# From the third batch on, attention 1's scores are turned by VectorE and a trip through DRAM instead of by TensorE

## The chip, the cores and the metric

The program runs on one core of a Trainium2 chip. The metric is the device time of one launch in microseconds (us), the median of a few runs. A core has TensorE (PE in the profile), VectorE (DVE), ScalarE (ACT), GpSimd (POOL) and SyncE (SP, which here only issues DMAs), each with its own instruction stream that runs in order and waits on semaphores of the others.

## The reference

Eight batches, eight heads, 576 positions of width 64, and 32 "pack" queries p. Attention 1 lets the pack queries look at k and v; attention 2 lets q look at the 32 packed rows; the result goes through a two-layer feed-forward net with softplus.

```
def sm_attn(qq, kk, vv):
    s = scale * np.matmul(qq, kk.transpose(0, 1, 3, 2))
    a = np.exp(s - np.max(s, axis=-1, keepdims=True))
    a = a / (np.sum(a, axis=-1, keepdims=True) + 1e-09)
    return np.matmul(a, vv)
p_packed = sm_attn(p, k, v)                 # attention 1: [8, 8, 32, 64]
out = sm_attn(q, p_packed, p_packed)        # attention 2: [8, 8, 576, 64]
x = out.transpose(0, 2, 1, 3).reshape(4608, 512)
h = x @ w_in                                # 512 x 2048
g = np.maximum(h, 0.0) + np.log1p(np.exp(-np.abs(h)))
return g @ w_out                            # 2048 x 512
```

## The kernel before

**Units.** The feed-forward net of a batch is done in 16 units f = 0 to 15, one for each 128 columns of the hidden layer. Batches are numbered from 0, as in the tiles' names: `a_5_1` is batch 5, group 1. In a unit TensorE runs 12 products of the first layer (`gemm1`, L744, six into each of the two halves `ph_f_0` and `ph_f_1`, c = 0 and 1, of 288 columns), then four tiles of the second layer (`acc_0` to `acc_3`, L810, three products each) that belong to the unit two before. ScalarE makes Abs, Exp and Ln of each half (L770 to L772), VectorE adds max(h, 0) (`e`, L787), which also frees that half of `ph` (there are two such banks, so the next unit's `gemm1` waits for it), and then splits the result into `gh` (L756) and `gl` (L757).

**Attention in slots.** The attention of batch b is done inside the units of batch b-1. `attention_in_slots` puts each step at a place (f, t): in unit f, behind tile `acc_t` (t = 0 to 3), or at t = END, behind the whole unit. This order is written out by hand for TensorE, VectorE and ScalarE. The eight heads form two groups g of four; the scores of a group lie in `a1[g]`, 128 partitions (4 heads x 32 pack rows) x 576 positions.

For one group the steps are: `move` turns k (`T_k`) or q (`T_q`, L299, VectorE in blocks of 32 x 32); `score1` (L318) multiplies; `max1` (L343) and `exp1` (L350) on VectorE and ScalarE; `turn1` (`a1_transposed`) turns the 128 x 576 scores into `a1T`, 96 positions on the partitions, by six TensorE transposes (`psa`, L363, three to a bank, c = 0 and 1) that ScalarE copies out (L364); `pack` (L377) multiplies `a1T` by v, 24 small products for each group; `scale_pack` (`pp`, L387) and `turn_pack` (`psx`, L392, and `pt`, L394) prepare the packed rows; `score2` at (6, END) and (10, END) starts attention 2.

For batches 3 to 7 the places are: `turn1` of group 0 at (2, 0) and (2, 2); `max1` and `exp1` of group 1 at (4, 0); `turn1` of group 1 twice at (4, END); `pack` at (5, 0), `scale_pack` at (5, 1), `turn_pack` at (5, 3). Batch 2 (`LATE`) starts later: its four `turn1` stand at (4, 0), (4, 2) and twice at (4, END). Batches 0 and 1 have an order of their own.

**Loads.** SyncE issues all loads and most stores. A load waits for its buffer (four `ld` buffers serve k, v and q in turn), and what stands behind it on SyncE waits too.

Of the kernel before, what the change touches and what calls it, by code (L numbers as in the profile page):

```python
# [9 lines left out]
F32 = mybir.dt.float32  # L10
# [16 lines left out]
def pack_attention_then_softplus_ffn(  # L27
# [10 lines left out]
    nc = tc.nc  # L38
    B, H, S, D = q.shape
    J = p.shape[2]  # L40
    DM, DFF = w_in.shape
    P = 128
    NP = 96
    SI = S // NP
    HS = SI // 2
    C = S // 2
    G = H * J // P
    HG = H // G
# [5 lines left out]
    LATE = 2  # L54
# [12 lines left out]
    cv = ctx.enter_context(tc.tile_pool(name="cv", bufs=1))  # L67
    work = ctx.enter_context(tc.tile_pool(name="work", bufs=2))
    small = ctx.enter_context(tc.tile_pool(name="small", bufs=2))
    ps_acc = ctx.enter_context(tc.tile_pool(name="ps_acc", bufs=NT, space=bass.MemoryType.PSUM))  # L70
    ps_h = ctx.enter_context(tc.tile_pool(name="ps_h", bufs=2, space=bass.MemoryType.PSUM))
    ps_m = ctx.enter_context(tc.tile_pool(name="ps_m", bufs=2, space=bass.MemoryType.PSUM))
# [20 lines left out]
    def bank(nm, pool=None):  # L93
        if pool:
            return pool.tile([P, 512], F32, tag="h", name=nm)
        if spare:
            spare.append(spare.pop(0))
            pool, tag = spare[-1]
            return pool.tile([P, 512], F32, tag=tag, name=nm)
        return ps_m.tile([P, 512], F32, tag="m", name=nm)  # L100
# [20 lines left out]
    loaded = {}  # L121
    late = []

    def load(nm, b, g):
        if b >= B:
            return
        if late is not None and b == LATE:
            late.append((nm, b, g))
            return
        with tc.issue_after(last_weight.ins) if b == LATE else nullcontext():  # L130
            load_now(nm, b, g)

    def load_now(nm, b, g):

        src = {"q": q, "k": k, "v": v}[nm][b, g * HG:(g + 1) * HG]
        if b < BY_BLOCK:
            t = ld.tile([NP, HG, SI, D], F32, tag="ld", name=f"{nm}_{b}_{g}")
            nc.sync.dma_start(
                t.rearrange("x h s d -> x h (s d)"), src.rearrange("h (x s) d -> x h (s d)", s=SI)
            )  # L140
        elif nm == "v":
            t = ld.tile([NP, HG, SI, D], F32, tag="ld", name=f"{nm}_{b}_{g}")
            nc.sync.dma_start(
                t.rearrange("x h s d -> x (h s) d"), src.rearrange("h (s x) d -> x (h s) d", s=SI)
            )
        else:
            t = ld.tile([P, HG, NB, J], F32, tag="ld", name=f"{nm}_{b}_{g}")
            blocks = src.rearrange("h (n c x) (w d) -> c w x (h n) d", c=2, x=J, w=D // J)
            for o in range(P // J):
                c, w = divmod(o, D // J)  # L150
                nc.sync.dma_start(
                    t[o * J:(o + 1) * J].rearrange("x h n d -> x (h n) d"), blocks[c, w]
                )
        loaded[nm, b, g] = t
# [16 lines left out]
    def release():  # L171

        nonlocal late
        late, todo = None, late
        for x in todo:
            load(*x)

    last_weight = None
# [180 lines left out]
    def a1_transposed(b, g, c, a1, a1T, copy=nc.scalar.copy):  # L359
        ps = bank(f"psa_{b}_{g}_{c}")  # L360
        for i in range(HS):
            o = c * C + i * NP
            nc.tensor.transpose(ps[:NP, i * P:(i + 1) * P], a1[:, o:o + NP], ident)  # L363
        copy(  # L364
            a1T[:, c * HS:(c + 1) * HS, :].rearrange("x s j -> x (s j)"), ps[:NP, :HS * P]
        )

    def packed(b, g, a1T, rs):

        ps = bank(f"psp_{b}_{g}")  # L370
        pack_products(b, g, a1T, ps)
        return pack_scaled(b, g, ps, rs)

    def pack_products(b, g, a1T, ps):
        for s in range(SI):
            for hh in range(HG):
                nc.tensor.matmul(  # L377
                    ps[hh * J:(hh + 1) * J, :D],
                    a1T[:, s, hh * J:(hh + 1) * J],
                    loaded["v", b, g][:, hh, 2 * (s % HS) + s // HS if b < BY_BLOCK else s, :],  # L380
                    start=(s == 0), stop=(s == SI - 1),
                )

    def pack_scaled(b, g, ps, rs):
        pp = small.tile([P, 2, D], F32, tag="pp", name=f"pp_{b}_{g}", bufs=2)
        for i in range(2):
            nc.vector.tensor_scalar_mul(pp[:, i, :], ps[:, :D], rs)  # L387
        return pp
# [128 lines left out]
    def attention_in_slots(b):  # L517

        kT, qT = {0: [], 1: []}, {0: [], 1: []}
        a1, nm, rs, a1T, pp, a2 = {}, {}, {}, {}, {}, {}  # L520

        def at(f, t, fn, *args):
            steps.setdefault(((b - 1) * NF + f, t), []).append((fn, args))
# [21 lines left out]

        def turn1(g, c):
            if c == 0:
                pool, tag, bufs = (cv, "x", 2) if g and b >= LATE else (work, "a1T", 1)
                a1T[g] = pool.tile([NP, SI, P], F32, tag=tag, name=f"a1T_{b}_{g}", bufs=bufs)
            a1_transposed(b, g, c, a1[g], a1T[g])  # L550

        def pack():
            pp["ps"] = bank(f"psp_{b}")
            for g in range(G):
                pack_products(b, g, a1T[g], pp["ps"][:, g * D:])
# [21 lines left out]
        END = NT  # L577
        if b < LATE:
            for g in range(G):
                for hh in range(HG):  # L580
                    at(1 + 2 * g + (2 * hh + 2 * g) // NT, (2 * hh + 2 * g) % NT, move, "k", g, hh)
                    at((6 if g else 7) + (4 * g) + hh // 2, hh % 2 * 2, move, "q", g, hh)
                at(3 + 2 * g, 1, score1, g, False)
                at(3 + 2 * g, 1, load, "q", b, g)
                at(3 + g, 0, load, "v", b, g)
                at(4 + 2 * g, 0, max1, g)
                at(4 + 2 * g, 0, exp1, g)
                at(5 + 2 * g, 0, sum1, g)
            for g in range(G):
                for c in range(2):  # L590
                    at(6 + g, (g + 2 * c) % NT, turn1, g, c)
                at(7 + g, 0, pack_one, g)
                at(8, 2, load, "k", b + 1, g)
                at(9, g, turn_pack, g)
                at(9 if g == 0 else 12, 3 if g == 0 else 1, score2, g, False)
                at(9 if g == 0 else 12, 3, load, "v", b + 1, g)
            at(10, 0, exp2, 0, 0)
            at(10, 0, exp2, 0, 1)
            at(10, 3, div2, 0, 0)
            at(11, 1, div2, 0, 1)  # L600
            at(13, 0, exp2, 1, 0)
            at(13, 0, exp2, 1, 1)
            at(13, 3, div2, 1, 0)
            at(14, 1, div2, 1, 1)
            return
        early = b == LATE
        if early:
            moves = ((0, 1), (0, 2), (0, 3), (1, 0)), ((2, 0), (2, 0), (2, 1), (2, 3))
        else:
            moves = ((-4, 1), (-3, 1), (-2, 1), (-2, 3)), ((0, 1), (0, 3), (2, 0), (2, 1))  # L610
        turns = ((2, END), (2, END), (3, 1), (4, 1)), ((8, 1), (9, 1), (10, 1), (10, 3))
        for what, places in (("k", moves), ("q", turns)):
            for g in range(G):
                for hh, place in enumerate(places[g]):
# [4 lines left out]
        if early:  # L619
            at(1, 3, score1, 0, False)  # L620
            at(1, 3, load, "q", b, 0)
            n = 3
        else:
            at(-2, END, score1, 0)
            at(-2, END, load, "q", b, 0)
            n = 0
        at(*((n, 1) if early else (1, 0)), max1, 0)
        at(*((n, 1) if early else (1, 1)), exp1, 0)
        n = 4 if early else 2
        at(n, 0, sum1, 0)  # L630
        at(n, 0, turn1, 0, 0)
        at(n, 2, turn1, 0, 1)
        at(4, 0, max1, 1)
        at(4, 0, exp1, 1)
        at(5, 0, sum1, 1)
        at(4, END, turn1, 1, 0)
        at(4, END, turn1, 1, 1)
        at(5, 0, pack)
        for g in range(G):
            at(5, 0, load, "k", b + 1, g)  # L640
            at(5, 1, scale_pack, g)
            at(5, 3, turn_pack, g)
        for g in range(G):
            f = 6 + 4 * g
            at(f, END, score2, g)
# [179 lines left out]
    def out_tile(nm):  # L825
        return cv.tile([P, 2, DM], F32, tag="x", name=f"o_{nm}", bufs=2)
# [80 lines left out]
    for b in range(BY_BLOCK, B):  # L907
        attention_in_slots(b)
    for u in range(len(units) + LAG):
        if u == NF:  # L910
            loads.close()
        if u < len(units):
            b, f = units[u]
# [26 lines left out]
        last = u >= LAG and f2 == NF - 1 and b2 % 2 == 1  # L940
# [4 lines left out]
        for t in range(NT):  # L945
# [4 lines left out]
            if last and t == 0:  # L950
                o = out_tile(f"{b2}_{t}")
# [20 lines left out]
            if u >= LAG and f2 == NF - 1:  # L972
                if t % 2 == 0 and not (last and t == 0):
                    o = out_tile(f"{b2}_{t}")
# [14 lines left out]
        if u + 2 < len(units):  # L989


            nb, c = units[u + 2][0], units[u + 2][1] * P
# [31 lines left out]
```

## Time and profile before

| | |
|---|---|
| time, median of 3 runs | 743.14 us (742.16 to 745.47) |
| span of the profiled execution, first to last instruction | 740.6 us |
| mean granted TensorE clock in it | 0.998 of full speed |
| TensorE busy | 723.8 us, 98% |
| VectorE busy | 533.0 us, 72% |
| ScalarE busy | 459.8 us, 62% |
| DMA | 55.97 MB, mean 76 GB/s |

The profiled execution's own time is not given apart; its span is 2.5 us below the median of the runs. In the profile "busy" of TensorE counts matmuls whose ends are modelled, so a distance between starts says more than a duration. Idle time stands in square brackets with what ended it.

### The profile page before, as it was taken

Reading aid. Unit: us, or ns where it says so; the run is one execution under the profiler, and the core shown is the slowest. Engines: PE = TensorE matmul, PEld = TensorE weight load, DVE = VectorE, ACT = ScalarE, POOL = GpSimd, SP = SyncE. Lnnn points to the kernel's source line nnn. Section 1 sums busy time; section 2 is a strip of 40 time slices with the busy share of each in tenths; the row PEclk is TensorE's granted clock in tenths of the full one; section 3 lists DMA queues with packets and bytes.
Section 4 is the critical chain, followed back from the end, with each engine's and each line's share of the span. In section 5 each row is a group of like instructions: output and inputs, shape, how many; then the busy total and the mean of one; then the engine's idle time right before and its main releaser. Section 6 shows DMA issues by size and latency. Waiting matters only on the chain.

```text
span 740.6 us, 14337 instructions
## 1 busy us (share of the span) xinstructions
PE 723.8 (98%) x5384; PEld 581.0 (78%) x5384; DVE 533.0 (72%) x1255; ACT 459.8 (62%) x1067; POOL 90.7 (12%) x166
## 2 busy tenths in 40 slices
PE   9889999999999999999999999999999999999997
PEld 7556766788887888888888788888888888888886
DVE  3889888678885588766886678875887658865553
ACT  3688897676563665775663655675664556665551
POOL 0235453000000000000000000000000000001110
PEclk9999999999999999999999999999999999999999
DMA  9999995560223501253121431235121200010002
GB/s 220 223 231 213 236 230 88 105 109 6 47 47 89 89 10 33 42 113 65 33 33 63 79 61 33 33 89 97 33 33 58 47 2 0 1 58 1 1 1 71
DMA packets 180197, 55.97 MB, mean 76 GB/s; under 512 B 167072, under 2 KB 169376, under 8 KB 180128
## 3 DMA queue, kind: packets, MB, share of 16 engines
q1 hardware_dynamic: 179504, 54.80, 35.2%
q8 instruction: 42, 0.69, 0.4%
q10 hardware_dynamic: 624, 0.26, 0.1%
q14 instruction: 27, 0.22, 0.1%
HBM read 45.61 MB, written 9.44 MB: 74 GB/s over the span
## 4 chain that ended last, share of the span: by engine, by line
PE 84%; DVE 7%; DMA 3%; ACT 3%; issue 1%; SPq 1%; POOL 1%; DVEq 0%; ACTq 0%; POOLq 0%
PE acc L810 42%; PE ph L744 25%; PE acc_m L810 6%; PE psm L697 3%; PE ps L318 2%; PE acc L807 2%; DMA v<-in_v 2%; PE psa L363 1%; PE psp L377 1%; DMA x_i<-in_moe_w_in 1%; POOL m L247 1%; DVE gl L757 1%; DVE e L787 1%; ACT e L770 1%; ACT e L771 1%
## 5 line engine op out<-in xcount | busy, mean ns | idle before, releaser
L810 PE MATMUL acc<-wo,gh 128*128 128x512 f32 x984 | 307.6, 394 | 0.0
L810 PEld LDWEIGHTS acc<-wo,gh 128*128 128x128 f32 x984 | 176.3, 188 | 31.2 <-issue 0.9
L770 ACT ACTIVATE e<-ph 128x288 f32<-128x288 f32 x256 | 102.1, 403 | 151.3 <-PE ph L744 145.9
L810 PE MATMUL acc<-wo,gl 128*128 128x512 f32 x492 | 192.6, 392 | 0.0
L787 DVE SCALAR_TENSOR_TENSOR e<-ph,e 128x288 f32<-128x288 f32 (+1 forms) x251 | 111.2, 447 | 101.9 <-ACT e L772 99.2
L744 PE MATMUL ph<-at_h,mh 128*128 128x288 f32 x512 | 157.3, 308 | 2.0 <-ACT at_h L334 1.5
L744 PE MATMUL ph<-at_h,ml 128*128 128x288 f32 x512 | 151.0, 296 | 1.3 <-DVE ml L719 1.3
L744 PE MATMUL ph<-at_l,mh 128*128 128x288 f32 x512 | 148.4, 296 | 2.7 <-DVE at_l L661 2.7
L744 PEld LDWEIGHTS ph<-at_h,mh 128*128 128x128 f32 x512 | 96.5, 188 | 34.8 <-DVE a L403 10.5
L796 POOL COPY rest<-e 128x64 f32<-128x64 f32 x128 | 49.1, 383 | 565.4 <-DVE e L787 564.7
L771 ACT ACTIVATE e<-e 128x288 f32<-128x288 f32 (+1 forms) x242 | 111.0, 459 | 7.7
L772 ACT ACTIVATE e<-e 128x288 f32<-128x288 f32 (+1 forms) x242 | 111.0, 459 | 7.7
L810 PEld LDWEIGHTS acc<-wo,gl 128*128 128x128 f32 x492 | 92.4, 188 | 19.9
L744 PEld LDWEIGHTS ph<-at_l,mh 128*128 128x128 f32 x512 | 95.5, 189 | 6.5 <-DVE at_l L661 3.6
L744 PEld LDWEIGHTS ph<-at_h,ml 128*128 128x128 f32 x512 | 96.5, 188 | 1.8 <-DVE ml L719 1.5
L757 DVE TENSOR_TENSOR gl<-e,gh 128x512 fp32r<-128x512 f32 x123 | 85.2, 693 | 8.7 <-DVE gh L756 0.5
L718 ACT CAST mh<-psm 128x512 fp32r<-128x512 f32 (+1 forms) x72 | 35.1, 540 | 39.9 <-PE psm L697 39.2
L756 DVE CAST gh<-e 128x512 fp32r<-128x512 f32 x123 | 51.9, 422 | 6.0
L719 DVE TENSOR_TENSOR ml<-psm,mh 128x512 fp32r<-128x512 f32 (+1 forms) x72 | 42.0, 625 | 15.6 <-ACT mh L718 15.6
L810 PE MATMUL acc_m<-wo,gh_m 128*128 128x512 f32 x128 | 39.8, 392 | 0.0
L697 PE MATMUL psm<-w_in_sb,pt 64*32 64x512 f32 (+1 forms) x576 | 39.1, 553 | 0.4 <-POOL w_in_sb L247 0.4
L810 PEld LDWEIGHTS acc_m<-wo,gh_m 128*128 128x128 f32 x128 | 23.8, 188 | 5.9 <-DVE gh_m L756 1.3
(91 smaller groups left out, 657.4 us busy)
## 6 DMA issues: line engine op xcount, KB each, us to landing
v<-in_v SPq DMA_DIRECT2D x16, 576.0 KB, 5.8
x_i<-in_moe_w_in SPq DMA_DIRECT2D x32, 256.0 KB, 7.7
x_o<-in_moe_w_out SPq DMA_DIRECT2D x16, 512.0 KB, 7.0
k<-in_k SPq DMA_DIRECT2D x56, 144.0 KB, 3.2
q<-in_q SPq DMA_DIRECT2D x56, 144.0 KB, 3.2
out<-o SPq DMA_DIRECT2D x28, 256.0 KB, 2.2
k<-in_k SPq DMA_DIRECT2D x2, 576.0 KB, 6.9
q<-in_q SPq DMA_DIRECT2D x4, 288.0 KB, 12.1
```

What stands on the lines that cost most here:

```text
L697: nc.tensor.matmul(ps[hh * J:(hh + 1) * J, :n], res["pt"][g][o:o + D, hh * J:(hh + 1) * J], w_in_sb[o:o + D, hh, c * n:(c + 1) * n], start ...
L718: nc.scalar.copy(mh[:, cols], ps[:, :n])
L719: nc.vector.tensor_tensor(ml[:, cols], ps[:, :n], mh[:, cols].bitcast(F32), op=ALU.subtract)
L744: nc.tensor.matmul(phs[c], x[:, o:o + P], y[:, g, cs], start=(i == mine[0]), stop=(i == mine[-1]),)
L756: nc.vector.tensor_copy(hi, x)
L757: nc.vector.tensor_tensor(lo, x, hi.bitcast(F32), op=ALU.subtract)
L770: nc.scalar.activation(es[c], hv[c], AF.Abs)
L771: nc.scalar.activation(e[:, x], e[:, x], AF.Exp, scale=-1.0)
L772: nc.scalar.activation(e[:, x], e[:, x], AF.Ln, bias=1.0)
L787: nc.vector.scalar_tensor_tensor(to[:, c * C + lo:c * C + hi], hv[c][:, lo:hi], 0.0, es[c][:, lo:hi], op0=ALU.max, op1=ALU.add,)
L796: nc.gpsimd.tensor_copy(rest[:, rest_at(b, f), r:r + REST], e[:, NT * P:])
L810: nc.tensor.matmul(acc, x[:, cs], y[f], start=(first and i == 0), stop=(last and i == 2),)
```

## The change

For batches 2 to 7 `turn1` is replaced by `spread1` (`a1_spread`). VectorE turns the scores of a group in blocks of 32 x 32, three instructions of 128 x 192 (one for each third o of 96 positions) into `aB`. SyncE writes each `aB` to a DRAM tile (`aD`, 128 rows of 768 bytes), and then reads the three back so that 32 positions of all four heads lie on 32 partitions of `a1T`. The DMAs are put in order behind one another: writes of a group, its reads, then any later load.

`aB` takes the tag "aT" of attention 2's weights, which has four buffers. The rest moves around it: `spread1` of group 0 at (3, 0), `max1` and `exp1` of group 1 from (4, 0) to (3, 1), `spread1` of group 1 at (4, 0); `pack` from (5, 0) to (5, 3), `scale_pack` from (5, 1) to (6, 0), `turn_pack` from (5, 3) to (6, 1); the first four turns of q later, to (4, 1) to (5, 3). In batch 2 both `spread1` stand at (4, 0).

```
+    dram = ctx.enter_context(tc.tile_pool(name="dram", bufs=G, space=bass.MemoryType.DRAM))
...
-        with tc.issue_after(last_weight.ins) if b == LATE else nullcontext():
+        with tc.issue_after(last_weight.ins) if b == LATE else behind_spread():
...
+    def a1_spread(b, g, a1):
+        Q = NP // J
+        pool, tag, bufs = (cv, "x", 2) if g else (work, "a1T", 1)
+        a1T = pool.tile([NP, HG, SI * J], F32, tag=tag, name=f"a1T_{b}_{g}", bufs=bufs)
+        froms = []
+        for o in range(Q):
+            aB = work.tile([P, SI * J], F32, tag="aT", name=f"aB_{b}_{g}_{o}", bufs=2 * G)
+            nc.vector.transpose(
+                aB.rearrange("p (s j) -> p s j", j=J),
+                a1.rearrange("p (s q x) -> p q s x", q=Q, x=J)[:, o],
+            )
+            to = dram.tile([HG, J, SI * J], F32, tag=f"a1_{o}", name=f"aD_{b}_{g}_{o}")
+            with behind_spread():
+                nc.sync.dma_start(to.rearrange("h x c -> (h x) c"), aB)
+            froms.append(to)
+        for o, to in enumerate(froms):
+            with behind_spread():
+                last = nc.sync.dma_start(a1T[o * J:(o + 1) * J], to.rearrange("h x c -> x h c"))
+        nonlocal last_spread
+        last_spread = last
+        return a1T
...
-                    a1T[:, s, hh * J:(hh + 1) * J],
+                    a1T[:, hh, s * J:(s + 1) * J] if b >= LATE
+                    else a1T[:, s, hh * J:(hh + 1) * J],
...
-        turns = ((2, END), (2, END), (3, 1), (4, 1)), ((8, 1), (9, 1), (10, 1), (10, 3))
+        turns = ((4, 1), (4, 3), (5, 1), (5, 3)), ((8, 1), (9, 1), (10, 1), (10, 3))
...
-        at(n, 0, turn1, 0, 0)
-        at(n, 2, turn1, 0, 1)
-        at(4, 0, max1, 1)
-        at(4, 0, exp1, 1)
+        at(4 if early else 3, 0, spread1, 0)
+        at(3, 1, max1, 1)
+        at(3, 1, exp1, 1)
+        at(4, 0, spread1, 1)
         at(5, 0, sum1, 1)
-        at(4, END, turn1, 1, 0)
-        at(4, END, turn1, 1, 1)
-        at(5, 0, pack)
+        at(5, 3, pack)
...
-            at(5, 1, scale_pack, g)
-            at(5, 3, turn_pack, g)
+            at(6, 0, scale_pack, g)
+            at(6, 1, turn_pack, g)
```

TensorE at the end of unit 4, attention of batch 5, before (`psa` are the transposes of group 1's scores, `ph_5` the first layer of unit 5):

```order
L810 MATMUL acc_2_5095<-wo_816,gh_2_5130 128x512 x2
L810 MATMUL acc_2_5095<-wo_816,gl_2_5131 128x512
L810 MATMUL acc_3_5096<-wo_816,gh_2_5130 128x512 x2
L810 MATMUL acc_3_5096<-wo_816,gl_2_5131 128x512
L363 MATMUL psa_1_0_5265<-ident,a_5_1_5134 96x128 x3
L363 MATMUL psa_1_1_5270<-ident,a_5_1_5134 96x128 x3
L744 MATMUL ph_5_0_5275<-at_h_4869,mh_1_0_5166 128x288
```

and with the change:

```order
L841 MATMUL acc_2_5127<-wo_818,gh_2_5151 128x512 x2
L841 MATMUL acc_2_5127<-wo_818,gl_2_5152 128x512
L841 MATMUL acc_3_5128<-wo_818,gh_2_5151 128x512 x2
L841 MATMUL acc_3_5128<-wo_818,gl_2_5152 128x512
L775 MATMUL ph_5_0_5313<-at_h_4901,mh_1_0_5183 128x288
```

The six transposes between the last tile of unit 4 and unit 5's first layer are gone; so are the two groups of three in unit 2.

VectorE in unit 4 of batch 2's attention, before (`rs` belongs to `sum1`, `m` and `nm` to `max1` of group 1, `e_4` frees the first half of `ph_4`; what an instruction waits for stands in brackets, DMAHW are DMA queues' semaphores):

```order
L355 TENSOR_SCALAR rs_0_2068<-z_2_0_2025 128x1
L356 RECIPROCAL rs_0_2068<-rs_0_2068 128x1 [waits DVE_49]
L343 TENSOR_REDUCE m_2_1_2077<-a_2_1_1951 128x1
L345 TENSOR_SCALAR nm_2_1_2079<-m_2_1_2077 128x1 [waits DVE_49]
L787 SCALAR_TENSOR_TENSOR e_4_2058<-ph_4_0_2044,e_4_2058 128x288 [waits Activation_49,Pool_49]
```

and with the change:

```order
L362 RECIPROCAL rs_0_2070<-rs_0_2070 128x1 [waits DVE_49]
L389 STREAM_TRANSPOSE aB_0_0_2074<-a_2_0_1873 128x192
L389 STREAM_TRANSPOSE aB_0_1_2078<-a_2_0_1873 128x192
L389 STREAM_TRANSPOSE aB_0_2_2082<-a_2_0_1873 128x192
L389 STREAM_TRANSPOSE aB_1_0_2090<-a_2_1_1953 128x192
L389 STREAM_TRANSPOSE aB_1_1_2094<-a_2_1_1953 128x192 [waits DMAHW0_49,DVE_49]
L389 STREAM_TRANSPOSE aB_1_2_2098<-a_2_1_1953 128x192 [waits DMAHW1_49,DVE_49]
L818 SCALAR_TENSOR_TENSOR e_4_2060<-ph_4_0_2046,e_4_2060 128x288 [waits Activation_49,Pool_49]
```

All six turns stand ahead of `e_4`, and the fifth and sixth wait for a DMA: with four buffers they take those of `aB_0_0` and `aB_0_1`, whose writes to DRAM (queues DMAHW0 and DMAHW1, below) must have landed.

SyncE at the same place, before (the last load ahead of it and the first behind it):

```order
L151 DMA q_1_1964<-in_q 32x36x32 [waits DMAHW7_49]
L151 DMA k_0_2198<-in_k 32x36x32 [waits DMAHW1_49,DMAHW0_49,DVE_49]
L151 DMA k_0_2198<-in_k 32x36x32
L151 DMA k_0_2198<-in_k 32x36x32 [waits DMAHW2_49]
L151 DMA k_0_2198<-in_k 32x36x32 [waits DMAHW3_49]
```

and with the change:

```order
L395 DMA aD_0_0_2076<-aB_0_0_2074 128x192 [waits DMAHW0_49,DVE_49]
L395 DMA aD_0_1_2080<-aB_0_1_2078 128x192 [waits DMAHW1_49,DVE_49]
L395 DMA aD_0_2_2084<-aB_0_2_2082 128x192 [waits DMAHW2_49,DVE_49]
L108 DMA p_2881<-in_p 32x8x64 [waits DMAHW3_49,Pool_49]
L399 DMA a1T_0_2073<-aD_0_0_2076 32x4x192 [waits DMAHW4_49,DMAHW0_49]
L399 DMA a1T_0_2073<-aD_0_1_2080 32x4x192 [waits DMAHW5_49,DMAHW1_49]
L399 DMA a1T_0_2073<-aD_0_2_2084 32x4x192 [waits DMAHW6_49,DMAHW2_49]
L395 DMA aD_1_0_2092<-aB_1_0_2090 128x192 [waits DMAHW7_49,DVE_49]
```

Twelve DMAs (and two quarters of a later load of p) stand between q and the next batch's k; each read waits for the landing of its write, and the writes of group 1 stand behind the reads of group 0.

## Rows read from the trace of the kernel before

**Rows 1.** The page: busy time by engine, granted clock in 40 slices, chain by engine.
```profile
PE 723.8 (98%) x5384; PEld 581.0 (78%) x5384; DVE 533.0 (72%) x1255; ACT 459.8 (62%) x1067; POOL 90.7 (12%) x166
...
PEclk9999999999999999999999999999999999999999
...
PE 84%; DVE 7%; DMA 3%; ACT 3%; issue 1%; SPq 1%; POOL 1%; DVEq 0%; ACTq 0%; POOLq 0%
```

**Rows 2.** Timeline, TensorE, an ordinary unit: start us, us, engine, line, out<-in, count.
```profile
439.32 0.62 PE L810 MATMUL acc<-wo,gh 128*128 128x512 f32 x2
...
440.01 0.62 PE L810 MATMUL acc<-wo,gh 128*128 128x512 f32 x2
...
443.65 0.62 PE L810 MATMUL acc<-wo,gh 128*128 128x512 f32 x2
```

**Rows 3.** Timeline, TensorE, attention of batch 5, units 2, 4 and 5.
```profile
406.38 0.62 PE L810 MATMUL acc<-wo,gh 128*128 128x512 f32 x2
...
407.32 0.71 PE L810 MATMUL acc<-wo,gh 128*128 128x512 f32 x2
...
408.10 0.62 PE L810 MATMUL acc<-wo,gh 128*128 128x512 f32 x2
...
417.44 0.62 PE L810 MATMUL acc<-wo,gh 128*128 128x512 f32 x2
...
420.32 0.86 PE L363 MATMUL psa<-ident,a 128*96 128x128 f32 x6
422.62 0.63 PE L810 MATMUL acc<-wo,gh 128*128 128x512 f32 x2
```

**Rows 4.** Timeline, TensorE, attention of batch 3, units 4 and 5.
```profile
245.25 0.63 PE L810 MATMUL acc<-wo,gh 128*128 128x512 f32 x2
...
249.04 0.86 PE L363 MATMUL psa<-ident,a 128*96 128x128 f32 x6 [0.89 <-ACT a L350]
...
251.33 0.63 PE L810 MATMUL acc<-wo,gh 128*128 128x512 f32 x2
```

**Rows 5.** Timeline, TensorE, attention of batch 2, units 4 and 5.
```profile
151.26 0.62 PE L810 MATMUL acc<-wo,gh 128*128 128x512 f32 x2
...
155.04 0.90 PE L363 MATMUL psa<-ident,a 128*96 128x128 f32 x6 [0.19 <-ACT a L350]
...
157.36 0.63 PE L810 MATMUL acc<-wo,gh 128*128 128x512 f32 x2
```

**Rows 6.** Timeline, VectorE, attention of batch 5, unit 3.
```profile
412.14 1.29 DVE L719 TENSOR_TENSOR ml<-psm,mh 128x512 fp32r<-128x512 f32 x2 [0.57 <-ACT mh L718]
414.02 0.46 DVE L787 SCALAR_TENSOR_TENSOR e<-ph,e 128x288 f32<-128x288 f32 x1 [0.60 <-ACT e L772]
...
415.21 0.46 DVE L787 SCALAR_TENSOR_TENSOR e<-ph,e 128x288 f32<-128x288 f32 x1 [0.34 <-ACT e L772]
...
416.17 0.69 DVE L757 TENSOR_TENSOR gl<-e,gh 128x512 fp32r<-128x512 f32 x1
```

**Rows 7.** Groups of VectorE by form: count | busy us, mean ns | idle before.
```profile
L299 DVE STREAM_TRANSPOSE T_q<-q 128x288 f32<-128x288 f32 x56 | 25.5, 463 | 4.1 <-PE ps L318 2.7 <-PE ph L744 1.5
...
L343 DVE TENSOR_REDUCE m<-a 128x1 f32<-128x576 f32 x16 | 11.9, 741 | 0.1
```

**Rows 8.** The line of the stores: ns to issue (min/median/max), us to landing.
```profile
L840 SPq DMA_DIRECT2D out<-o x36: 332/362/1457, 136.6 to 725.9; - x36
...
DMA to landing us min/median/max: 2.0/2.3/4.1
```

**Rows 9.** The page's DMA issues: count, KB each, median us from issue to landing.
```profile
k<-in_k SPq DMA_DIRECT2D x56, 144.0 KB, 3.2
...
p<-in_p SPq DMA_DIRECT2D x6, 64.0 KB, 2.3
```

**Rows 10.** Timeline, VectorE, attention of batch 2, unit 4: `sum1` of group 0.
```profile
152.51 0.16 DVE L356 RECIPROCAL rs<-rs 128x1 f32<-128x1 f32 x1
```

More of the change, by code (lines that the diff above doesn't have):

```diff
@@ L122, in pack_attention_then_softplus_ffn, with behind_spread @@
     late = []
+    last_spread = None
+    def behind_spread():
+        return tc.issue_after(last_spread.ins) if last_spread else nullcontext()
     def load(nm, b, g):
@@ L547, in turn1, with spread1 @@
             if c == 0:
-                pool, tag, bufs = (cv, "x", 2) if g and b >= LATE else (work, "a1T", 1)
-                a1T[g] = pool.tile([NP, SI, P], F32, tag=tag, name=f"a1T_{b}_{g}", bufs=bufs)
+                a1T[g] = work.tile([NP, SI, P], F32, tag="a1T", name=f"a1T_{b}_{g}", bufs=1)
             a1_transposed(b, g, c, a1[g], a1T[g])
+        def spread1(g):
+            a1T[g] = a1_spread(b, g, a1[g])
         def pack():
```

## The prediction

> **What bounds the kernel now.** I read the busy times first: TensorE 98%, VectorE 72%, ScalarE 62%, and TensorE's granted clock at the full 2.4 GHz level in every slice; then the chain that ends last, of which TensorE is 84% [rows 1]. So the time is TensorE's stream, and an edit is worth what it changes in the distance between TensorE's own starts. For that I took the timeline of TensorE. In an ordinary unit a tile of the second layer follows the one before by 0.69 us, and the first tile of the next unit comes 4.33 us after the first of this one [rows 2]; the first layer's 12 products are the rest, 4.33 - 4 x 0.69 = 1.57. Below, S4 is the start of unit 4's first layer, that is 1.57 before its first tile, and so on; in S3 + x the time counts from the start of unit 3.
>
> **What is taken off TensorE.** Each group of three transposes between two tiles costs: first tile to second 407.32 - 406.38 = 0.94, so 0.25 over 0.69; and the tile behind starts its successor 0.78 later, 0.09 over (its weights come late) [rows 3]. That is 0.34. The six at the end of unit 4 are seen as unit 4's length, 422.62 - 417.44 = 5.18, so 0.85 over 4.33 [rows 3]. In batch 3 the same place is 251.33 - 245.25 = 6.08, so 1.75 over, since there TensorE waits 0.89 for the exponentials, which stand late on ScalarE [rows 4]. In batch 2 all four groups lie in one unit: 157.36 - 151.26 = 6.10, so 1.77 over [rows 5]. The sum: batch 2 1.77; batch 3 1.75 + 2 x 0.34 = 2.43; batches 4 to 7, all like batch 5, 4 x (0.85 + 0.68) = 6.12. **Together 10.3 us.** ScalarE loses 24 copies of the turned scores, which were not on the path; I cost that at nothing. Pack and the two `psx` transposes only change their place: as many instructions on TensorE between the same neighbours.
>
> **What is put on VectorE.** 36 turns of 128 x 192. The nearest row is the turn of 128 x 288 at 0.46 [rows 7]; by columns it would be 0.31, and the read is strided, so I take 0.35 and keep 0.31 and 0.46 as the ends. Where does it meet TensorE? TensorE needs the first half of `ph` back at S4 and the second one when its first six products are done, S4 + 0.8. In batch 5 S3 is 411.5. The `ml` subtractions end at 413.43, S3 + 1.9; ScalarE lets the two `e` steps start at S3 + 2.5 and S3 + 3.7 at the earliest [rows 6]. Now three turns follow `ml`: S3 + 2.95; the first `e` (0.46) to 3.4; `max1`, moved here, 0.74 [rows 7] and 0.15 for its scaling, to 4.3; the second `e` to 4.75. TensorE asks for it at S3 + 4.33 + 0.8 = 5.1. So 0.35 is left, nothing is lost, and at 0.46 a turn it just comes out even. The turns of q that were in unit 3 go to units 4 and 5, where VectorE has room. Steps `gh` and `gl` (0.43 and 0.69) end at S3 + 5.85, that is S4 + 1.5, and then the three turns of group 1 start; the first `e` of unit 4 then is done by S4 + 3.05, asked for at S5 = S4 + 4.33. The moved `scale_pack` waits for nothing longer than before, and `pt` is ready some 0.5 us ahead of `score2`. I cost all this at nothing in batches 3 to 7.
>
> **The trip.** Let L be the time from issue to landing. A store takes 0.36 to issue and lands after 2.0 to 4.1, median 2.3; a load of 64 KB in rows of 256 bytes 2.3, one of 144 KB in rows of 128 bytes 3.2 [rows 8, 9]. A leg here has 96 KB in rows of 768 bytes; I take L = 2.3, with 0.4 for an issue, and keep 2.0 and 3.2 as ends. In batches 3 to 7: first turn of group 1 done at S4 + 1.9, writes issued at 1.9, 2.3, 2.7, the last read issued when the last write has landed, so the scores are there at S4 + 2.75 + 2L = S4 + 7.35. Pack stands behind unit 5's tiles, S4 + 8.66, and its second half, which alone needs group 1, 0.78 later at 9.44. So there are 2 us to spare, up to L = 3.35. Group 0 is a unit ahead. What is queued behind the waiting reads on SyncE is k of the next batch, needed eight units later, and nothing else soon.
>
> **Batch 2 pays.** There both groups turn at once. `sum1` of group 0 ends at 152.67 [rows 10]; the first turn is done at 153.0, the next at 153.4, and their writes go out then. The fifth turn needs the buffer of the first and waits for its write, the sixth for the second write: 153.4 + L = 155.7, so the sixth is done at 156.05, and only then comes `e` of unit 4, done at 156.5. TensorE wants that half at S5 = 151.26 - 1.57 + 4.33 = 154.0. **It waits 2.5.** Then SyncE: the reads of group 0 end their issue when the third write (153.8) has landed, the writes of group 1 go behind them, then their reads: 155.0 + 3L = 161.9 against pack's second half at 156.5 + 4.33 + 0.78 = 161.6. **Another 0.3.** So batch 2 loses 2.8, and 3 us more for each us of L above 2.3.
>
> **The sum**: -10.3 + 2.8 = -7.5. The profiled span, 740.6, becomes 733.1; the 2.5 between span and median stays, and 743.14 becomes **735.6 us**. With L = 2.0 it is 734.7, with L = 3.2 batch 2 costs 5.5 and it is 738.3.
>
> **Rivals.**
> (1) Batch 2 does not stall (landings sooner, or TensorE late there for its own reasons): 743.14 - 10.3 = 732.8. Against it: VectorE runs in order and the wait is in its list.
> (2) The trip is slow, the case on the other side. Its place is the first product of pack's second half, in every batch; it begins at L = 3.35, costs 2 us per us of L in each of five batches and 3 in batch 2. It eats the whole gain at L = 3.7, and is slower by 0.5% from 4.0. With the longest landing of a store, 4.1 [rows 8], batch 2 costs 8.2 and the others 5 x 1.5, so 743.14 - 10.3 + 15.7 = 748.5. For it: reads wait on fresh writes, which no row shows, and the writes follow a load of q in the same queue. Against it: the medians, and a DMA load that is low in these units.
> (3) VectorE becomes the bound. A turn of over 0.47 delays the second `e` of unit 3, 3 us per us, and over 0.66 also the first of unit 4. At twice the 288-column turn, 0.93: 1.4 + 0.8 = 2.2 in each of five batches and some 1.2 in batch 2, so 743.14 - 7.5 + 12.2 = 747.8. For it only the strided read speaks. The Trainium skill has a rule against the change as such: the page "VectorE: DVE Perf Modes", section "Rules for kernel authors", would leave the turn of a whole tile to TensorE where the result may lie in PSUM, and give VectorE only blocks of 32 x 32; by it the kernel before has the better path, and the time would be 743 or more. The rule compares the paths one by one; the trace here has TensorE at 98% and VectorE at 72% [rows 1], so I give it no more than this rival's chance.
> (4) Small waits of some 0.5 to 1 us a batch that I don't see (a landing now and then, a DMA behind q's): 738 to 742.
> That the change does not do what it says is out: the transposes of batches 2 to 7 are gone from TensorE's list.
>
> **How the numbers follow.** The forecast has 0.64, with its own range 734.5 to 738.5; (1) 0.10; (2) 0.12; (3) 0.08; (4) 0.06. A measurement of this kernel can tell about 0.5%, 3.7 us, from no change: faster is below 739.4, slower above 746.9. Faster: nearly all of the forecast (0.63), (1), and a third of (4): 0.75. Of (2) a little over half and of (3) less than half lie above 746.9: 0.10. The rest, 0.15, is within. The range for 8 in 10 takes in (1), the forecast and (4): 732.5 to 742.
>
> **What would show it.** Right: unit 2 of batches 3 to 7 shorter by 0.68, unit 4 by 0.85 (batch 3 by 1.75); TensorE's first layer of unit 5 in batch 2's attention waiting some 2.5 for `e`; pack without a wait on a DMA in batches 3 to 7, landings of both legs near 2.3, turns near 0.35. Wrong: `psp` waiting for `a1T` in every batch (rival 2), `ph` of units 4 or 5 waiting for `e` in every batch (rival 3), or a second half of the trip much longer than the first.

## The result, and the profile after

| | median | lowest to highest | runs |
|---|---|---|---|
| kernel before | 744.31 us | 742.16 to 746.26 | 4 |
| changed kernel | 735.69 us | 734.89 to 735.94 | 4 |

The ratio is 0.988, with a 95% interval of 0.986 to 0.990: the change makes the kernel 1.2% faster. The profiled execution of the changed kernel took 735.94 us, the longest of its four; its span is 734.2 us.

From the page of the changed kernel, the busy times and the granted TensorE clock in 40 slices; they answer to [rows 1]:

```profile
PE 715.9 (98%) x5312; PEld 575.7 (78%) x5312; DVE 542.1 (74%) x1291; ACT 450.7 (61%) x1043; POOL 89.8 (12%) x166
PEclk9989999999999999999999999999999999999999
```

TensorE has lost 7.9 us of busy time and VectorE has gained 9.1; both shares have hardly moved, so TensorE is still the bound. Where the time went is seen in the distances between TensorE's own starts. I take a unit as the distance from its first `gemm1` product to the next unit's, read off TensorE's timeline, and add units up by stage; the attention of batch b lies in the stage of batch b-1.

| stage (its attention) | before | changed | difference |
|---|---|---|---|
| 0 (batch 1) | 95.46 | 97.21 | +1.75 |
| 1 (batch 2) | 83.63 | 84.19 | +0.56 |
| 2 (batch 3) | 93.11 | 90.80 | -2.31 |
| 3 to 6 (batches 4 to 7) | 341.87 | 335.63 | -6.24 |
| 7 (none) | 68.69 | 68.69 | 0 |

So batches 3 to 7 gain 8.55, batch 2 loses 0.56, and this profile has 1.75 in stage 0, where the change does nothing. That stage is looked at below. Inside batches 4 to 7 it is unit 2 that became shorter (6.61 to 5.92), unit 4 (5.08 to 4.33), and units 5 and 6, between which pack and the `psx` transposes moved (6.26 to 5.90, 6.03 to 6.29, together 0.10 less). In batch 3 unit 4 went from 6.08 to 4.41.

**Batch 5**, which stands for 3 to 7. VectorE's timeline, the columns being start, duration, engine, line, operation and tiles, and in brackets the idle time and what ended it; it answers to [rows 6]:

```profile
410.92 0.88 DVE L389 STREAM_TRANSPOSE aB<-a 128x192 f32<-128x192 f32 x3
411.73 0.42 DVE L818 SCALAR_TENSOR_TENSOR e<-ph,e 128x288 f32<-128x288 f32 x1
...
412.90 0.45 DVE L818 SCALAR_TENSOR_TENSOR e<-ph,e 128x288 f32<-128x288 f32 x1
...
414.45 0.89 DVE L389 STREAM_TRANSPOSE aB<-a 128x192 f32<-128x192 f32 x3
415.95 0.46 DVE L818 SCALAR_TENSOR_TENSOR e<-ph,e 128x288 f32<-128x288 f32 x1 [0.61 <-ACT e L803]
```

SyncE's issues in the same place, and TensorE's tiles and pack, which answer to [rows 3]:

```profile
411.31 1.30 SPq L395 DMA_DIRECT2D aD<-aB  x3
413.00 1.27 SPq L399 DMA_DIRECT2D a1T<-aD  x3
414.86 1.29 SPq L395 DMA_DIRECT2D aD<-aB  x3
416.52 1.27 SPq L399 DMA_DIRECT2D a1T<-aD  x3
```

```profile
415.03 0.62 PE L841 MATMUL acc<-wo,gh 128*128 128x512 f32 x2
...
419.35 0.62 PE L841 MATMUL acc<-wo,gh 128*128 128x512 f32 x2
...
422.19 1.55 PE L407 MATMUL psp<-v,a1T 96*32 96x64 f32 x96
```

Unit 4 from first tile to first tile is now 4.32, the length of an ordinary unit, where it was 5.18. The second `e` of unit 3 ends at 413.35; TensorE asks for it 0.8 behind S4, at 415.03 - 1.57 + 0.8 = 414.26, so 0.9 is to spare. The last read is issued at about 417.5 and takes 2.0 to land, so the scores lie ready at 419.5; pack's second half, 0.78 behind its first, comes at 422.97. That is 3.5 us to spare, and pack runs through as one row of 96.

The two legs, from issue to landing (smallest, median, largest), writes first:

```profile
DMA to landing us min/median/max: 1.6/1.7/1.9
```

```profile
DMA to landing us min/median/max: 1.9/2.0/2.7
```

**Batch 2**, first VectorE, then TensorE, then SyncE; these answer to [rows 5] and [rows 10]:

```profile
154.27 1.14 DVE L389 STREAM_TRANSPOSE aB<-a 128x192 f32<-128x192 f32 x4
156.39 0.84 DVE L389 STREAM_TRANSPOSE aB<-a 128x192 f32<-128x192 f32 x2 [0.98 <-DMA aD<-aB]
157.15 0.42 DVE L818 SCALAR_TENSOR_TENSOR e<-ph,e 128x288 f32<-128x288 f32 x1
```

```profile
155.34 0.39 PE L841 MATMUL acc<-wo,gl 128*128 128x512 f32 x1
157.62 0.40 PE L775 MATMUL ph<-at_h,mh 128*128 128x288 f32 x1 [1.90 <-DVE e L818]
...
162.16 0.88 PE L407 MATMUL psp<-v,a1T 96*32 96x64 f32 x48
163.19 0.88 PE L407 MATMUL psp<-v,a1T 96*32 96x64 f32 x48 [0.15 <-issue]
```

```profile
154.65 1.30 SPq L395 DMA_DIRECT2D aD<-aB  x3
156.05 0.38 SPq L108 DMA_DIRECT2D p<-in_p  x1
156.53 1.35 SPq L399 DMA_DIRECT2D a1T<-aD  x3
157.97 1.33 SPq L395 DMA_DIRECT2D aD<-aB  x3
159.34 0.45 SPq L108 DMA_DIRECT2D p<-in_p  x1
159.90 1.34 SPq L399 DMA_DIRECT2D a1T<-aD  x3
```

VectorE makes four turns and then stands 0.98 until a write of `aD` has landed: the first write is issued at 154.65 and 1.7 later, at 156.35, its buffer is free. The `e` that TensorE waits for stands behind the sixth turn. TensorE's last tile of unit 4 starts at 155.34, its successor would start 0.23 later, and it starts at 157.62: 2.05 late. Pack's second half starts 1.03 behind the first instead of 0.78: another 0.25. The bracket there names no releaser ("issue"), but the last read is issued at 160.86 and lands 2.1 later, at 162.95, and the product starts 0.24 behind that; in two runs below, where the bracket names the DMA ("other buffers" and "pack early"), it starts 0.25 behind the landing.

### The profile page after: what moved, and what is told of

The parts are those of the page before. It is cut to its first block, busy times and chain, and to the rows that moved or that the text cites. A ratio compares the mean times of both kernels' runs of the same rounds, so it can differ in the third digit from the quotient of the medians.

```text
span 734.2 us, 14362 instructions
## 1 busy us (share of the span) xinstructions
PE 715.9 (98%) x5312; PEld 575.7 (78%) x5312; DVE 542.1 (74%) x1291; ACT 450.7 (61%) x1043; POOL 89.8 (12%) x166
## 4 chain that ended last, share of the span: by engine, by line
PE 87%; DMA 5%; ACT 3%; DVE 3%; SPq 1%; issue 1%; POOL 0%; DVEq 0%; ACTq 0%
PE acc L841 43%; PE ph L775 28%; PE acc_m L841 6%; DMA x_i<-in_moe_w_in 4%; PE psm L728 4%; PE ps L324 3%; PE acc L838 2%; PE psp L407 1%; DMA k<-in_k 1%; SPq L157 1%; ACT m L236 1%; ACT r L237 0%; ACT e L801 0%; ACT e L802 0%; DVE e L818 0%
```

## The experiments

My theory: the gain is the transposes taken off TensorE, minus nothing in batches 3 to 7, minus batch 2's two waits, of which the first comes from four buffers for six turns. Rivals: the gain comes from the earlier exponentials; the trip or VectorE costs something hidden in every batch; the wait in batch 2 has another cause. One table for all runs, stage lengths read as above; "3-7" is the sum of the five stages with the attention of batches 3 to 7.

| kernel | time | span | stage 0 | batch 2 | 3-7 |
|---|---|---|---|---|---|
| before, again | 742.26 | 740.2 | 95.49 | 83.46 | 434.88 |
| changed, again | 735.91 | 734.1 | 95.93 | 85.34 | 426.48 |
| other buffers in batch 2 | 735.21 | 733.4 | 95.51 | 84.25 | 426.49 |
| batch 2 earlier | 734.07 | 730.6 | 95.49 | 81.79 | 426.46 |
| exponentials early, transposes kept | 741.16 | 739.2 | 95.50 | 83.19 | 433.03 |
| no trip | 732.9 | 730.3 | 95.47 | 81.82 | 426.42 |
| one more copy in DRAM | 763.87 | 762.0 | 95.46 | 91.08 | 448.49 |
| turns three times | 754.71 | 752.9 | 95.50 | 89.28 | 441.89 |
| pack early | 737.56 | 735.8 | 95.90 | 86.60 | 426.61 |

"Changed, again" and "batch 2 earlier" are medians of four runs; the others are one run each. Spans and stages are of the one profiled execution.

### Both kernels again

> The kernel before, word for word, for a second profile. Theory: the attention of batches 2 to 7 is done in the same unit lengths again, to 0.1 us; what differs between two profiles (the changed kernel had batch 0's stage 1.75 us longer than the kernel before) is the weight loading stage, which varies from execution to execution. Rival: batch 0's stage is the same in both profiles of this kernel, to 0.3 us; then the change itself makes that stage longer.

> The changed kernel, word for word. Theory: 735.7, batches 2 to 7 in the same unit lengths as in its first profile, batch 2's unit 4 again near 6.6. Batch 0's stage anywhere within 2 us of the first profile; if it is again 1.75 longer than that of the kernel before, the change costs something there that the prediction had not.

Before: all stages as in the first profile to within 0.2. Changed: 735.91 (735.63 to 736.45) against 743.43 for before on the same chip (7 runs, 743.3 to 744.18), ratio 0.990 [0.988, 0.991]. Batches 3 to 7 repeat to 0.05. Stage 0 took 95.93, so the 97.21 of the first profile belongs to that execution and not to the change. Batch 2, though, took 85.34 instead of 84.19, with the same wait of TensorE:

```profile
156.39 0.40 PE L775 MATMUL ph<-at_h,mh 128*128 128x288 f32 x1 [1.90 <-DVE e L818]
```

The 4 us from 158 on, first in this execution, then in the first profile; columns: stretch, its length, busy time of PE, PEld, DVE, ACT and POOL with their instructions, the granted clock, DMA share, GB/s:

```profile
158.00:162.00 4.00, 4.00 (x16) 3.43 (x16) 3.83 (x11) 2.96 (x7) 0.24 (x1) 0.70 0.51 144
```

```profile
158.00:162.00 4.00, 4.00 (x24) 3.39 (x22) 3.83 (x11) 3.01 (x7) 0.24 (x1) 1.00 0.67 196
```

Behind the same wait TensorE ran at 2.4 GHz throughout in one execution, and partly at 1.2 GHz in the other, where the next unit took 7.57 instead of 6.38: 1.2 us more. So batch 2's stall has a second price that is not paid in every execution. Where it was paid, pack came so late that its second half had nothing left to wait for:

```profile
162.47 1.56 PE L407 MATMUL psp<-v,a1T 96*32 96x64 f32 x96
```

### What makes batch 2 wait

Two edits. The first gives the fifth and sixth turn two buffers of another tag:

```
-            aB = work.tile([P, SI * J], F32, tag="aT", ..., bufs=2 * G)
+            tag, bufs = ("a2", 2) if b == LATE and g and o else ("aT", 2 * G)
+            aB = work.tile([P, SI * J], F32, tag=tag, ..., bufs=bufs)
```

> In batch 2 the fifth and sixth turn take buffers of another tag, which are idle there, so VectorE waits for no write. Theory: the six turns still stand ahead of the activation step (6 x 0.28 = 1.7 from 154.3 on), so TensorE's wait at unit 5 falls from 2.0 to about 0.9, and pack's second half, whose data hang on SyncE's order and not on the turns, waits about 1.3 instead of 0.25: net within 0.2 of the changed kernel. Rival: the buffer wait is the whole cost of batch 2; then batch 2 gets shorter by 1.0 to 1.2.

```profile
153.43 1.66 DVE L390 STREAM_TRANSPOSE aB<-a 128x192 f32<-128x192 f32 x6
155.01 0.42 DVE L819 SCALAR_TENSOR_TENSOR e<-ph,e 128x288 f32<-128x288 f32 x1
```

```profile
155.49 0.40 PE L776 MATMUL ph<-at_h,mh 128*128 128x288 f32 x1 [0.60 <-DVE e L819]
...
160.02 0.88 PE L408 MATMUL psp<-v,a1T 96*32 96x64 f32 x48
162.41 0.88 PE L408 MATMUL psp<-v,a1T 96*32 96x64 f32 x48 [1.51 <-DMA a1T<-aD]
```

VectorE (first rows) makes its six turns without a gap, and TensorE's wait for `e` falls from 1.90 to 0.60. Unit 4 is 1.29 shorter than in the first profile of the changed kernel. But pack then asks sooner for data that land as late as before, since the four groups of DMAs stand one behind the other on SyncE: its second half waits 1.51, unit 5 is 1.35 longer, and batch 2 ends 0.06 later. So the buffers caused 1.3 us of the first wait. The 0.60 that is left goes with the six turns that still stand ahead of `e`; it is gone in the next run, where only three do. More buffers alone are worth nothing against the first profile. Against the second one, where the clock fell, batch 2 is 1.09 shorter here; one execution of this kernel doesn't tell how often the clock would fall in it.

The second edit starts batch 2 a unit earlier, so that the two groups no longer turn in one place:

```
-        at(*((n, 1) if early else (1, 0)), max1, 0)
-        at(*((n, 1) if early else (1, 1)), exp1, 0)
-        n = 4 if early else 2
+        at(*((2, 1) if early else (1, 0)), max1, 0)
+        at(*((2, 1) if early else (1, 1)), exp1, 0)
+        n = 3 if early else 2
...
-        at(4 if early else 3, 0, spread1, 0)
+        at(3, 0, spread1, 0)
```

> In batch 2 the maximum and exponential of group 0 go from (3, 1) to (2, 1) and its turn from (4, 0) to (3, 0), as in the later batches. Theory: no wait at unit 5 and none at pack; batch 2's units 4 to 6 get shorter by 2.0 + 0.25, some 2.2 in all, 733.5. If VectorE has no room in units 2 and 3 of batch 2 (turns of k stand there), up to 1 us of it comes back as a wait of the first layer for the activation step. Rival: the wait only moves, to unit 3 or 4; then no gain.

```profile
147.97 0.88 DVE L389 STREAM_TRANSPOSE aB<-a 128x192 f32<-128x192 f32 x3
...
152.56 0.89 DVE L389 STREAM_TRANSPOSE aB<-a 128x192 f32<-128x192 f32 x3
```

```profile
158.99 1.56 PE L407 MATMUL psp<-v,a1T 96*32 96x64 f32 x96
```

Now three turns lie in unit 3 and three in unit 4, and TensorE waits neither at unit 5 nor at pack (last row). Batch 2 takes 81.79: 2.40 less than in the first profile of the changed kernel (unit 4 -2.27, unit 5 -0.47, unit 2 +0.39), 3.55 less than in the second, where the clock fell. The time is 734.07 us (732.42 to 734.46), the ratio to before 0.987 [0.986, 0.989]. This is the best complete kernel here: its four runs lie below all four of the changed kernel on the same chip (735.63 to 736.45), by 1.8 at the medians. The intervals of the two ratios still touch, so the size of this last step is less sure than its place; and the profiled execution, 732.42, is at least 1.6 below the other three.

### What the gain of batches 3 to 7 is made of

The kernel before, with `max1` and `exp1` of group 1 and the turns of q where the change has them, and the TensorE transposes kept:

```
-        turns = ((2, END), (2, END), (3, 1), (4, 1)), ((8, 1), (9, 1), (10, 1), (10, 3))
+        turns = ((4, 1), (4, 3), (5, 1), (5, 3)), ((8, 1), (9, 1), (10, 1), (10, 3))
...
-        at(4, 0, max1, 1)
-        at(4, 0, exp1, 1)
+        at(3, 1, max1, 1)
+        at(3, 1, exp1, 1)
```

> The kernel before, with TensorE's transposes, but the maximum and exponential of group 1 at (3, 1) and the first turns of q at (4, 1) to (5, 3), as the change has them. Theory: only waits go: batch 3's unit 4 from 6.08 to about 5.15 (the 0.89 wait), batch 2's by about 0.2, batches 4 to 7 by at most 0.1 from 5.08; unit 2 stays at 6.6. In all 1.2 to 1.6 less than the kernel before. Rival: the earlier exponentials are what gains, and TensorE's transposes were hidden; then units 4 go to 4.33 without any trip.

Batches 3 to 7 take 433.03, 1.85 less than before: unit 4 of batch 3 -1.08, of the others -0.18 each (at most 0.1 was expected); unit 2 is unchanged. The six transposes at the end of batch 3's unit 4 no longer wait for the exponentials (0.89 in [rows 4]):

```profile
248.58 0.82 PE L363 MATMUL psa<-ident,a 128*96 128x128 f32 x6
```

In batch 5 the kernel before had such a wait too, on the transposes' weight load (PEld):

```profile
420.32 0.61 PEld L363 LDWEIGHTS psa<-ident,a 128*96 128x96 f32 x6 [0.40 <-ACT a L350]
```

The changed kernel saves 8.4 to 8.5 in these batches. So 1.8 of that comes from the steps that were moved and could have been had without any trip; the waits that went were for the exponentials, though the turns of q were moved in the same run and not tested alone. The other 6.6 goes with the transposes themselves.

Next, neither turns nor trip: pack multiplies one tile that is written once, so attention 1's scores don't reach the output.

```
     def a1_spread(b, g, a1):
+        if not still:
+            t = work.tile([NP, HG, SI * J], F32, tag="a1T", name="still", bufs=1)
...
+        return still[0]
```

> The changed kernel without the turns on VectorE and without the trip: from batch 2 on pack multiplies one tile that is written once (so the packed rows are not those of the scores). Theory: in batches 3 to 7 turns and trip cost nothing, so every unit stays within 0.1 us of the changed kernel; batch 2's units 4 and 5 lose their waits, 2.0 to 2.4 us. Rival: the trip costs something in every batch (a late landing, a late activation step); then units 2 to 6 of batches 3 to 7 get shorter too.

Batches 3 to 7 take 426.42, the changed kernel 426.43 and 426.48. The 30 turns and 60 DMAs of these five batches cost nothing that shows: the kernel before differs by 0.1 between its own two profiles. Batch 2 takes 81.82, which the kernel with batch 2 earlier reaches with all its work done (81.79), though not in the same places: there unit 2 is 0.39 longer than here (6.68 to 6.29), and units 4 and 5 together 0.39 shorter.

### How near the edge is

One more copy from DRAM to DRAM between the writes and the reads makes the trip longer by a leg:

```
+            on = dram.tile([HG, J, SI * J], F32, tag=f"a1_{o}_on", ...)
+            with behind_spread():
+                nc.sync.dma_start(on..., to...)
+            nexts.append(on)
+        for o, to in enumerate(nexts):
```

> The changed kernel with one more copy from DRAM to DRAM between the writes and the reads of every group. Theory: in the changed kernel batch 5's last read of group 1 lands 3.5 us before pack's second half. SyncE works in order, so the copy (2 us a leg) is paid once for group 0, whose reads hold up group 1's writes from 414.9 to about 416.4, and once for group 1: the data come about 4 us later than now, pack waits 0.5 (0 to 1.3) in batches 3 to 7 and about 4 more in batch 2; 738 to 746. Rival: a leg is hidden whatever its length, since pack stands late; then no wait in batches 3 to 7.

Of batch 5, VectorE's turns of group 1, SyncE's issues, TensorE around pack, and a stretch of 2 us behind it (the clock is the third figure from the end):

```profile
428.39 0.89 DVE L389 STREAM_TRANSPOSE aB<-a 128x192 f32<-128x192 f32 x3
```

```profile
429.13 1.74 SPq L407 DMA_DIRECT2D a1T<-aE  x3
431.23 1.33 SPq L395 DMA_DIRECT2D aD<-aB  x3
433.12 1.75 SPq L401 DMA_DIRECT2D aE<-aD  x3
435.30 3.00 SPq L407 DMA_DIRECT2D a1T<-aE  x3
```

```profile
436.12 0.88 PE L415 MATMUL psp<-v,a1T 96*32 96x64 f32 x48
440.07 0.88 PE L415 MATMUL psp<-v,a1T 96*32 96x64 f32 x48 [3.08 <-DMA a1T<-aE]
```

```profile
442.00:444.00 2.00, 2.00 (x10) 2.00 (x9) 0.00 (x0) 1.30 (x3) 0.00 (x0) 0.50 1.07 169
```

The place is the one that rival 2 of the prediction named: the first product of pack's second half, in every batch (waits of 1.46 to 3.08 in batches 3 to 7, 3.97 in batch 2). The size was not expected: 27.9 us more in the span, where I had reckoned with some 10 at most. Two terms were too small, and one was missing in the sum. First, the hold-up by the order on SyncE, put at 1.5 (414.9 to 416.4): group 1's turns begin at 428.39, and its writes could go out 0.41 later as in the changed kernel (414.45 to 414.86), but the reads of group 0, themselves a leg later, stand in front, and so they go out at 431.23, 2.4 late. Second, group 1's own way, put at some 2.5 more: from there to the landing it is 8.8 (to 440.0) instead of 4.6 (414.86 to 419.5), so 4.2 more. 2.4 + 4.2 - 3.5 of spare time is 3.1, and the wait is 3.08. Missing was the clock: about that wait it falls to 0.50, the 1.2 GHz level, in every batch, and units 5 and 6 of a batch together lose 3.2 to 5.7. Of the 22.0 that batches 3 to 7 lose, the five waits are 12.2; the rest goes with the low clock. Why the wait differs from batch to batch is not shown. That a leg is hidden whatever its length is false; and what is to spare is spent by both groups, since their DMAs share one queue.

Every turn issued three times:

```
+            for _ in range(3):
                 nc.vector.transpose(
```

> Each of the 36 turns on VectorE is done three times, so a group takes 2.6 us instead of 0.88. Theory: the second activation step of unit 3 has 0.9 us to spare in the changed kernel; 1.76 more makes TensorE wait 0.9 at unit 4 and, since unit 4's first activation step stands behind the three turns of group 1, some 0.8 at unit 5: 1.6 in each of batches 3 to 7, about 2 in batch 2; 744 to 748. Rival: VectorE is busy 74% of the time and takes it up; then nothing beyond batch 2.

```profile
420.44 3.37 DVE L390 STREAM_TRANSPOSE aB<-a 128x192 f32<-128x192 f32 x9
423.73 0.42 DVE L819 SCALAR_TENSOR_TENSOR e<-ph,e 128x288 f32<-128x288 f32 x1
```

```profile
424.20 0.40 PE L776 MATMUL ph<-at_h,mh 128*128 128x288 f32 x1 [1.07 <-DVE e L819]
...
430.22 0.40 PE L776 MATMUL ph<-at_h,mh 128*128 128x288 f32 x1 [1.00 <-DVE e L819]
```

TensorE (last rows) waits for `e` at the start of units 4 and 5 in every batch, as rival 3 has it. Nine turns into three tiles take 3.37 (0.37 each), where three take 0.88, so 2.49 a group is added and not the 1.76 that I had expected from the distance of 0.28 between turns into different tiles: each repeat into the same tile waits for the turn before it. In the changed kernel the first `e` of unit 3 ends at 412.15 and is asked for at S4 = 413.46, 1.3 later; 2.49 - 1.3 = 1.2 is what unit 3 loses (1.23), and unit 4 loses 1.70. So it is the first `e` that binds here, where I had named the second, and a batch loses 3.1 instead of 1.6; batch 2 loses 3.9 to 5.1 against about 2. The time, 754.71 us, lies above the 744 to 748 that I expected. The place was right; the price was too low.

Last, pack, its scaling and its turn back in the places that they had before:

```
-        at(5, 3, pack)
+        at(5, 0, pack)
...
-            at(6, 0, scale_pack, g)
-            at(6, 1, turn_pack, g)
+            at(5, 1, scale_pack, g)
+            at(5, 3, turn_pack, g)
```

> The changed kernel with pack, its scaling and its turn back at (5, 0), (5, 1) and (5, 3). Theory: in batch 5 the data land at 419.5 and pack's second half would come at 420.8, so batches 3 to 7 don't wait; their units 5 and 6 go back to 6.26 and 6.03 (together 0.1 longer). In batch 2 the data land about 2.2 after pack asks for them. In all 2.5 to 3 more than the changed kernel (up to 2 more where the granted clock falls after that wait). Rival: the landings need the later place; then pack waits in every batch, 0.5 us or more.

Pack in batch 2, on TensorE's timeline:

```profile
160.53 1.01 PE L407 MATMUL psp<-v,a1T 96*32 96x64 f32 x48
162.32 0.88 PE L407 MATMUL psp<-v,a1T 96*32 96x64 f32 x48 [0.78 <-DMA a1T<-aD]
```

In batch 5 pack runs through at its old place (96 products in 1.55 us from 421.66), and batches 3 to 7 take 426.61, 0.13 more than with pack late, about what two profiles of one kernel differ by: units 5 and 6 change back to 6.16 and 6.01 (12.17 together, 12.19 with pack late) and nothing waits. Against "exponentials early, transposes kept", which has pack in the same place, these batches take 6.4 less: that pair differs by the transposes against turns and trip alone. In batch 2 it waits 0.78, less than the 2.2 I expected, because TensorE came there late: the granted clock had been 0.64 in the 4 us from 158 on. Batch 2 is 1.26 longer than in "changed, again", where the clock fell too. The time, 737.56 us, is 1.7 above that of "changed, again", less than the 2.5 to 3 that I expected. So only batch 2 needs the later place of pack.

## Why the prediction came out right, step by step

It said 735.6 us for 743.14; measured were 735.69 and 735.91, against 744.31 and 743.43. The unit lengths show which of this is understanding and which is luck.

- **TensorE is the bound: right.** It stays at 98%, and every gain is seen as a shorter unit. One reading was loose: a 9 in the row of slices stands for 90% or more and not for the full level; in the kernel before the granted clock was 0.50 from 42 to 44 us, in stage 0, which the sum doesn't use.
- **What is taken off: right in size.** Unit 2 of batches 3 to 7 by 0.68 to 0.69 (0.68 predicted); unit 4 of batch 5, first tile to first tile, 5.18 to 4.32, so 0.86 (0.85). By stages batch 3 gains 2.31 (2.43), batches 4 to 7 6.24 (6.12): 8.55 against 8.55. Part of it was put down to the wrong thing: the prediction has the whole 0.85 as the price of six transposes, and of that 0.18 is had by moving the exponentials and q's turns alone; in batch 3 that move gives 1.08, where 0.89 was read as the wait. The move of pack and of the `psx` transposes, costed at nothing, is worth nothing that shows (units 5 and 6 12.19 with it, 12.17 without).
- **VectorE's spare time: right in sign, too small.** I took 0.35 for a turn; a single one shows 0.34, but three follow at 0.28. So 0.9 is left where I had worked out 0.35, and rival 3 was further off than I had it: three turns can take 0.9 more, so one could take 0.58, not 0.47, before the second `e` is late. The Trainium skill's rule that I set against the change (page "VectorE: DVE Perf Modes", section "Rules for kernel authors") would have led the wrong way for this kernel: with the transposes on the full engine, TensorE, batches 3 to 7 took 433.03 us, and with VectorE's turns and the trip 426.5, the exponentials standing alike. That doesn't make the new path the quicker one: one group's turns and trip take 5.0 us in batch 5 (414.45 to 419.5), its six transposes 0.86.
- **The trip: right in sign, too long.** I took 2.3 a leg from the medians of a store and of a load of p; measured are 1.7 and 2.0. With VectorE's turns 0.5 sooner the data land at S4 + 6.0 instead of S4 + 7.35, 3.5 ahead of pack instead of 2. Rival 2 did not come true, but its place was right: the run with one more copy waits just where it said. Its prices were too low: 2 us per us of L counted only group 1's own two legs, not group 0's ahead of them in SyncE's order, and not the fall of the clock about the wait.
- **Batch 2: the mechanism was right, both waits at their places.** 2.5 predicted, 2.05 measured; 0.3 predicted, 0.25 measured in the first profile and none in the second, where the clock had already made TensorE late. The first is smaller through the shorter leg. At the second the shorter leg made up for what I had left out: the two loads of p that SyncE issues in between (0.38 and 0.45), and the 0.24 from the landing to the product. What was missing is the clock: in one execution the same wait cost 1.2 more, in the other nothing beyond itself. Net of the 1.77 of transposes, batch 2 loses 0.56 in one profile and 1.88 in the other ("again" against "again"); predicted was 1.03.
- **Rivals.** Rival 1, no stall in batch 2, is what "no trip" and "batch 2 earlier" show: spans of 730.3 and 730.6. Rival 4, small waits in every batch, is out: 426.42 without the trip, 426.43 to 426.48 with it.
- **The sum** had -7.5. By the unit lengths of the first profile, without stage 0, it is -8.55 + 0.56 = -8.0; by those of the second -8.4 + 1.88 + 0.44 (stage 0) = -6.1, and the spans differ by 6.1 there (740.2 to 734.1). That the medians met the forecast to 0.1 is partly chance. Before measured 743.14 in the three runs that the prediction starts from, 744.31 with a fourth one and 743.43 in the second set, so that the time fell by 8.6 or by 7.5; the profiled execution of before in the second set, 742.26, was shorter than the seven others of that set. And the 2.5 between span and median joined the span of one execution to the median of others: within one execution the time is 1.7 to 2.1 above the span, with either kernel.

## What to carry to other kernels

Where one engine is the bound at 98%, a step that is taken off it is worth its share of the distance between that engine's starts, even if it comes back as a much longer way through an engine and queues that have time; what has to be worked out is when the result is asked for, and by how much it is early. Count the buffers of the new way against how many steps start in one place: four buffers for six turns put a DMA's landing in front of VectorE's next step, and TensorE paid for it; and look at what is late next before adding buffers, since the wait only went to pack. Split a change into what moves and what replaces: 1.8 of 8.4 us came from moves that needed no trip.

## What the runs showed of the hardware that I had not expected

- **A wait of TensorE of some 2 us has a second price, at times.** After the same wait of 1.90 us the granted clock stayed at 1.00 in one execution (unit 5 6.38 us) and went to a mean of 0.70 in the 4 us behind it in another (7.57 us); it also fell in "pack early", behind 1.90 (0.64 from 158 to 162). With one more copy, behind 3.08 us of waiting, it was 0.50 for a whole stretch of 2 us, and it fell in every batch, at a wait of 1.46 too. It did not fall behind 0.60 and 1.51 in one unit ("other buffers"), nor behind 1.07 and 1.00 ("turns three times": 1.00 from 424 to 431).
- **Stage 0 differs by execution.** It took 97.21 in the first profile of the changed kernel, and 95.46 to 95.93 in all other executions. Most of the 1.75 over before is in units 9 to 11 (1.3): TensorE waited 1.90 there for VectorE's `ml`, where it had waited 0.53. Another 0.4 is in units 0 to 3, where it waited 2.90 for `at_h` and the granted clock was low for longer, 0.55 from 44 to 48 us against 0.93 before. The first two rows are of the changed kernel, the third of the one before.

```profile
40.50 0.40 PE L775 MATMUL ph<-at_h,mh 128*128 128x288 f32 x1 [2.90 <-ACT at_h L340]
...
93.68 0.33 PE L423 MATMUL psx<-ident,pp 128*128 128x128 f32 x1 [1.90 <-DVE ml L750]
```

```profile
92.09 0.33 PE L392 MATMUL psx<-ident,pp 128*128 128x128 f32 x1 [0.53 <-DVE ml L719]
```

- **DMA legs through DRAM.** With 96 KB in rows of 768 bytes: 1.7 us to write, 2.0 to read back in another order, 2.4 from DRAM to DRAM; an issue on SyncE takes 0.33 to 0.38, and three from DRAM to DRAM 1.75 together.
- **A repeated turn waits for the one before it.** Turns of 128 x 192 follow each other at 0.26 to 0.30 into different tiles, with no idle time between. Repeated into the same tile ("turns three times") they follow at 0.37 to 0.41: the program has a wait for VectorE's own semaphore ahead of each repeat, and VectorE idles 0.035 there.
